# Attention and a gated MLP on one core: the attention weights are transposed under a second name typed fp32r

## The chip, the core and the metric

The program runs on one core of a Trainium2 chip. The metric is device time in microseconds (us) of one execution; lower is better. Engines are named as in the profile: PE is the matrix engine (TensorE), PEld its weight loads, DVE the vector engine, ACT the scalar engine, POOL is GpSimd, SP is the queue that issues DMAs.

## The reference

For 8 batches of 8 heads, with 576 positions and 64 dimensions a head, causal attention with a decay bias is computed, and the heads of a batch then go through a gated MLP:

```
scores = q @ k.T / sqrt(D)
cum    = cumsum(maximum(s, 0))
scores = where(causal, -1e9, scores + minimum(-(cum[i] - cum[j]), 0))
attn   = exp(scores - max(scores)); attn /= attn.sum() + 1e-9
x      = attn @ v                          # [8, 576, 512], heads side by side
h      = gelu(x @ w_in)                    # 512 -> 1024
u, v   = h[..., :512], h[..., 512:]
v_n    = layer_norm(v) * g_ln
out    = x + (u * (w_sg @ v_n + b_sg)) @ w_out
```

## The kernel before, in words

One head after the other goes through four steps, and the MLP of batch b is spread over the steps of the heads of batch b+1, so that PE has work of two kinds at any time.

1. *Scores* (L297 and L298 for heads 8 to 63, L295 for the first eight): five strips of query rows, `it` = 0 to 4, of 64, 192, 320, 448 and 576 columns, land in PSUM (`sc`). DVE adds the mask, scales, finds the row minimum and writes the strip to the SBUF tile `p_it` (L305). ACT takes the exponential in place and sums the row (L315).
2. *Normalization* (L338): POOL multiplies each strip by the reciprocal of its row sum, in place. Two small pieces go elsewhere: strip 0 (64x64) is written into columns 384 to 448 of `p_3`, and a 64x64 piece of strip 1 into columns 256 to 320 of `p_2`. For heads 0 to 11 ACT does strip 3 (L336).
3. *Transposes* (L377): PE transposes the strips in 13 pieces of 128x128 (one of them 128x64) into PSUM tiles `pt`, as four groups of 4, 4, 2 and 3. The data is the stationary operand and the identity moves: the profile writes `pt<-ident,p`. ACT (L88) and DVE (L93) take each group out of PSUM, as an fp32r high part and an fp32r rest (`pah`, `pal`, `pbh`, `pbl`, `pdh`, `pdl`). There are two sets of `p` tiles, for even and odd heads.
4. *Weights times values* (L450, L472; `xx`), added up by ACT and DVE into `xr`.

The MLP consists of units: `v` (L518, and L532 to L535 for the last 64 positions, which need the tile `xq` that a DMA copies from `xs`), `u` (L582), `s` (L597 to L601) and `o` (L616). All products are made of three fp32r products (high times high, high times rest, rest times high), except in the first 8 and 12 heads, where scores and values are plain fp32.

The order in which the steps are written is set by a table of times (`place`, `spread`). The order in which instructions then stand on each engine is set by the scheduler of the tile framework, which goes by its own estimates of durations; every engine runs its instructions in that order. The scheduler also places the waits: an instruction that reads a tile waits for the writers of what it reads.

Of the kernel before, what the change touches and what calls it, by code (L numbers as in the profile page):

```python
# [8 lines left out]
F32 = mybir.dt.float32  # L9
F32R = mybir.dt.float32r  # L10
# [10 lines left out]
P = 128  # L21
# [15 lines left out]
ITW = [64, 192, 320, 448, 576]  # L37
PW = [64, 192, 384, 512, 576]
# [21 lines left out]
def tile_attn_gmlp(  # L60
# [10 lines left out]
    out: bass.AP,  # L71
):
    nc = tc.nc

    const = ctx.enter_context(tc.tile_pool(name="const", bufs=1))
    att = ctx.enter_context(tc.tile_pool(name="att", bufs=2))
# [9 lines left out]
    def split(hi, lo, src, eng_hi, eng_lo):  # L86
        if eng_hi is nc.scalar:
            nc.scalar.copy(out=hi, in_=src)  # L88
        elif eng_hi is nc.gpsimd:
            nc.gpsimd.tensor_scalar(out=hi, in0=src, scalar1=1.0, scalar2=1.0, op0=ALU.mult, op1=ALU.mult)  # L90
        else:
            nc.vector.tensor_copy(out=hi, in_=src)
        eng_lo.tensor_tensor(out=lo, in0=src, in1=hi.bitcast(F32), op=ALU.subtract)  # L93
# [43 lines left out]
    for c0, n in ((0, 512), (512, REM)):  # L137
        ps = ps_sc.tile([P, 512], F32, name="cps", tag="sc")
# [10 lines left out]
    for i in range(WARM):  # L149
# [4 lines left out]
    nc.sync.dma_start(out=cum.rearrange("a h s -> h a s"), in_=cc[0:BH].bitcast(F32))  # L154


    ident = const.tile([P, P], F32, name="ident")
    nc.vector.memset(ident, 0.0)
    nc.gpsimd.affine_select(out=ident, in_=ident, pattern=[[1, P]], base=0, channel_multiplier=-1,
                            compare_op=ALU.not_equal, fill=1.0)  # L160
    mask = const.tile([P, 448], BF16, name="mask")
    nc.vector.memset(mask, 0.0)
# [4 lines left out]
    for r0, c in ((0, 512), (64, 448)):  # L167
        nc.gpsimd.affine_select(out=mask2[r0:r0 + 64, :], in_=mask2[r0:r0 + 64, :], pattern=[[-1, S]], base=c,
                                channel_multiplier=1, compare_op=ALU.is_ge, fill=NEG)
# [3 lines left out]


    q2 = []
    pbuf = []
    sums = []
    for i in range(2):
        t = const.tile([66, S], F32R, name=f"q2_{i}")
        nc.vector.memset(t[64:66, :].bitcast(F32), 1.0)  # L180
        q2.append(t)
        ts_ = []
        for it in range(5):
            t = const.tile([P, PW[it]], F32, name=f"p_{i}_{it}")
            if PW[it] > ITW[it]:
                nc.gpsimd.memset(t[:, ITW[it]:PW[it]], 0.0)
            ts_.append(t)
        pbuf.append(ts_)
        t = const.tile([P, 5], F32, name=f"sum_{i}")
        nc.vector.memset(t, 1.0)  # L190
        sums.append(t)
# [178 lines left out]

    def transposes(h):
        d = heads[h]
        pb = pbuf[h % 2]
        pt = {}

        def tr(ps, c, it, jb, n=P):
            nc.tensor.transpose(out=ps[0:n, c:c + P], in_=pb[it][:, jb:jb + n], identity=ident)  # L377

        def new(name, w):
            if h < NP:  # L380
                x = "hl"[h % 2]
                pt[name] = (att.tile([P, w], F32, name=name + x, tag=name + x, bufs=1),)
            else:
                pt[name] = tuple(att.tile([P, w], F32R, name=name + x, tag=name + x, bufs=1) for x in "hl")

        def evac(name, c0, ps, w, e=nc.scalar):
            if h < NP:
                o = pt[name][0][:, c0:c0 + w]
                (e.copy if e is nc.scalar else e.tensor_copy)(out=o, in_=ps[:, 0:w])  # L389
            else:  # L390
                hi, lo = (t[:, c0:c0 + w] for t in pt[name])
                split(hi, lo, ps[:, 0:w], nc.scalar, nc.vector)

        d["pt"] = pt
        t = ps_pt.tile([P, 512], F32, name="pt", tag="pt")
        for c, it in ((128, 3), (384, 2), (0, 1), (256, 4)):
            tr(t, c, it, 0)
        new("pa", 512)
        evac("pa", 0, t, 512)
        yield 0.43  # L400
        t = ps_pt.tile([P, 512], F32, name="pt", tag="pt")
        tr(t, 384, 3, 128)
        tr(t, 0, 3, 256)
        tr(t, 256, 2, 256)
        tr(t, 128, 4, 256)
        new("pb", 768)
        evac("pb", 0, t, 512, nc.vector)
        yield 0.43
        t = ps_pt.tile([P, 512], F32, name="pt", tag="pt")
        tr(t, 128, 2, 128)  # L410
        tr(t, 0, 4, 128)
        evac("pb", 512, t, 256)
        yield 0.43
        t = ps_pt.tile([P, 512], F32, name="pt", tag="pt")
        tr(t, 0, 4, 512, 64)
        tr(t, 64, 3, 384)
        tr(t, 192, 4, 384)
        if h < NP:
            pt["pd"] = (att.tile([P, 320], F32, name="pdh", tag="pdh", bufs=1),)
            nc.vector.tensor_copy(out=pt["pd"][0][0:64, 0:64], in_=t[0:64, 0:64])  # L420
            nc.vector.tensor_copy(out=pt["pd"][0][:, 64:320], in_=t[:, 64:320])
        else:
            hi, lo = pt["pd"] = tuple(att.tile([P, w], F32R, name="pd" + x, tag="pd" + x, bufs=1)
                                      for x, w in (("h", 320), ("l", 192)))
            nc.scalar.copy(out=hi[0:64, 0:128], in_=t[0:64, 0:128])
            nc.scalar.copy(out=hi[:, 128:320], in_=t[:, 128:320])
            nc.vector.tensor_tensor(out=hi[64:128, 0:128], in0=t[0:64, 0:128], in1=hi[0:64, 0:128].bitcast(F32),
                                    op=ALU.subtract)
            nc.vector.tensor_tensor(out=lo, in0=t[:, 128:320], in1=hi[:, 128:320].bitcast(F32), op=ALU.subtract)
        yield 0.35  # L430
# [205 lines left out]
    def advance(g, h):  # L636
        if h not in g[1]:
            g[1][h] = g[0](h)
        next(g[1][h], None)

    sc, tr, pp = (scores, {}), (transposes, {}), (pv, {})
    for h in range(BH):
        if h > 0:
# [25 lines left out]
    while steps:  # L669
        steps.sort()  # L670
        _, _, f, args = steps.pop(0)
# [53 lines left out]
```

## Time and profile before

| | |
|---|---|
| three timed runs | 827.47, 827.79, 828.27 us; median 827.79 |
| span of the profiled execution | 828.8 us, 1.0 us above that median |
| mean granted TensorE clock | 0.991 |
| PE busy | 792.6 us (96%) |
| DVE, ACT, POOL busy | 597.9 (72%), 576.5 (70%), 595.1 (72%) |
| L377, the transposes, on PE | 137.2 us in 832 instructions |

A PE record of a matmul is longer than the time that the matmul holds PE, since matmuls are pipelined; so the records overlap, and what a matmul costs a busy PE is read from the distance of the starts, or from the chain of waits, which gives each piece its share of the elapsed time. The chain follows back from the last instruction, at each step to whatever ended last.

### The profile page before, as it was taken

The numbers are of one execution on the slowest core, as the hardware profiler recorded it, in microseconds if no ns is written. First come the engines' busy times: TensorE is split into PE (matmuls) and PEld (weight loads), VectorE is DVE, ScalarE is ACT, GpSimd is POOL, SyncE is SP. The second block draws the span as 40 slices with busy tenths as digits, with TensorE's granted clock in tenths as the row PEclk, the third lists the DMA queues.
The fourth block names the chain that finished last, engine by engine and source line by source line (L and its number), as shares of the span: only waits on it lengthen the run. The fifth ranks groups of instructions, "written<-read, shape, count | busy, mean of one in ns | idle before, by whom it ended". The sixth has DMA issues, their size and how long they took to land.

```text
span 828.8 us, 16733 instructions
## 1 busy us (share of the span) xinstructions
PE 792.6 (96%) x5161; PEld 696.1 (84%) x5161; DVE 597.9 (72%) x1806; ACT 576.5 (70%) x1620; POOL 595.1 (72%) x979
## 2 busy tenths in 40 slices
PE   6899999899999999999989999999999999999878
PEld 3355666889989998999979998899989998899778
DVE  5995468975787578966888577965888678963652
ACT  4787778775686678866878577866787677862430
POOL 4987668878677768796768778785778778872451
PEclk9999999999999999999999999999999999999989
DMA  7656553343442543444434453443444353400101
GB/s 210 215 158 181 148 139 84 86 105 100 116 106 74 128 125 86 108 121 126 112 82 104 115 139 90 113 109 96 119 119 103 100 152 93 98 26 23 35 8 57
DMA packets 69804, 89.29 MB, mean 108 GB/s; under 512 B 25954, under 2 KB 42212, under 8 KB 69716
## 3 DMA queue, kind: packets, MB, share of 16 engines
q1 hardware_dynamic: 69716, 88.23, 40.8%
q8 instruction: 41, 0.67, 0.4%
q14 instruction: 47, 0.39, 0.2%
HBM read 42.27 MB, written 9.73 MB: 63 GB/s over the span
## 4 chain that ended last, share of the span: by engine, by line
PE 73%; DVE 12%; DMA 5%; ACT 3%; issue 3%; POOL 2%; SPq 1%; DVEq 0%; POOLq 0%; ACTq 0%
PE om L616 12%; PE sm L597 11%; PE um L582 10%; PE xx L450 10%; PE vm L518 9%; PE pt L377 8%; PE sc L297 4%; PE sc L298 4%; DVE p L305 2%; DMA xq<-xs 2%; DMA q<-k 2%; PE sm L601 1%; PE sm L600 1%; DVE wbits L220 1%; DVE vm L504 1%
## 5 line engine op out<-in xcount | busy, mean ns | idle before, releaser
L338 POOL TENSOR_SCALAR p<-p,rs 128x448 f32<-128x448 f32 (+4 forms) x372 | 180.5, 499 | 29.1 <-DVE rs L321 9.6
L315 ACT ACTIVATE p<-p,mn 128x448 f32<-128x448 f32 (+4 forms) x320 | 177.9, 557 | 24.5 <-DVE mn L305 22.4
L305 DVE CUSTOM_DVE_ANT_0 p<-sc,mask 64x64 f32<-64x64 f32 (+4 forms) x320 | 126.2, 422 | 56.4 <-PE pt L377 31.0
L377 PE MATMUL pt<-ident,p 128*128 128x128 f32 (+1 forms) x832 | 137.2, 278 | 5.3 <-DVE pbl L389 2.6
L597 PE MATMUL sm<-ws,vn 128*128 128x288 f32 x768 | 130.3, 304 | 0.7 <-POOL vn L567 0.6
L93 POOL TENSOR_TENSOR k<-raw,k 128x576 fp32r<-128x576 f32 x56 | 80.3, 1433 | 66.7 <-ACT k L88 33.3
L582 PE MATMUL um<-xs,wi 128*128 128x288 f32 x768 | 123.4, 300 | 2.5 <-DVE u L504 2.4
L616 PE MATMUL om<-gt,wo 128*128 128x288 f32 x768 | 125.7, 298 | 0.0
L582 PEld LDWEIGHTS um<-xs,wi 128*128 128x128 f32 x768 | 108.9, 188 | 8.9 <-DVE u L504 4.0
L597 PEld LDWEIGHTS sm<-ws,vn 128*128 128x128 f32 x768 | 112.4, 192 | 3.3 <-DVE u L504 1.0
L377 PEld LDWEIGHTS pt<-ident,p 128*128 128x128 f32 (+1 forms) x832 | 96.8, 138 | 21.8 <-DVE pbl L389 5.4
L616 PEld LDWEIGHTS om<-gt,wo 128*128 128x128 f32 x768 | 110.6, 188 | 2.3
L518 PE MATMUL vm<-wi,xs 128*128 128x512 f32 x384 | 103.4, 399 | 0.0
L297 PE MATMUL sc<-k,q 128*128 128x448 f32 x336 | 100.8, 308 | 1.5 <-DVE mn L305 0.8
L298 PE MATMUL sc<-k,q 66*128 66x448 f32 x336 | 89.3, 298 | 0.6 <-DMA k<-cum 0.6
L88 ACT CAST pbh<-pt 128x512 fp32r<-128x512 f32 x104 | 48.9, 479 | 58.8 <-PE pt L377 58.8
L518 PEld LDWEIGHTS vm<-wi,xs 128*128 128x128 f32 x384 | 69.7, 189 | 14.9 <-POOL xs L93 1.6
L93 POOL TENSOR_TENSOR gt<-u,gt 128x288 fp32r<-128x288 f32 x64 | 50.7, 806 | 41.6 <-ACT gt L88 41.1
L297 PEld LDWEIGHTS sc<-k,q 128*128 128x128 f32 x336 | 60.8, 181 | 9.1 <-DVE mn L305 3.9
L93 DVE TENSOR_TENSOR pbl<-pt,pbh 128x512 fp32r<-128x512 f32 x104 | 56.5, 549 | 15.9 <-ACT pbh L88 15.9
L298 PEld LDWEIGHTS sc<-k,q 66*128 66x128 f32 x336 | 60.9, 181 | 5.9 <-issue 0.9
L88 ACT CAST k<-raw 128x576 fp32r<-128x576 f32 x56 | 37.6, 671 | 39.5 <-PE sc L297 33.8
(142 smaller groups left out, 1704.8 us busy)
## 6 DMA issues: line engine op xcount, KB each, us to landing
q<-k SPq DMA_DIRECT2D x168, 144.0 KB
raw<-in_kq SPq DMA_DIRECT2D x56, 288.0 KB
vr<-in_vp SPq DMA_DIRECT2D x52, 192.0 KB
out_t<-ot SPq DMA_DIRECT2D x64, 144.0 KB
k<-k SPq DMA_DIRECT2D x56, 144.0 KB
wraw<-in_w_in SPq DMA_DIRECT2D x16, 256.0 KB
kf<-in_kq SPq DMA_DIRECT2D x8, 288.0 KB
qf<-in_kq SPq DMA_DIRECT2D x8, 288.0 KB
```

Of the source, the lines that this page charges most:

```text
L88: nc.scalar.copy(out=hi, in_=src)
L93: eng_lo.tensor_tensor(out=lo, in0=src, in1=hi.bitcast(F32), op=ALU.subtract)
L297: nc.tensor.matmul(o, d["q1"][:, i0:i0 + r], d["k1"][:, j0:j1], start=True, stop=False)
L298: nc.tensor.matmul(o, q2[h % 2][:, i0:i0 + r], d["k2"][0:66, j0:j1], start=False, stop=True)
L305: nc.vector.tensor_tensor_reduce(out=pbuf[h % 2][it][0:r, j0:j1], in0=pst[0:r, c0:c0 + j1 - j0], in1=(mask2 if it in (2, 4) else mask)[0:r ...
L315: nc.scalar.activation(out=p, in_=p, func=AF.Exp, bias=d["mn"][0:r, it:it + 1], scale=-1.0, accum_out=sums[h % 2][0:r, it:it + 1])
L338: e.tensor_scalar(out=po, in0=pi, scalar1=f, scalar2=1.0, op0=ALU.mult, op1=ALU.mult)
L377: nc.tensor.transpose(out=ps[0:n, c:c + P], in_=pb[it][:, jb:jb + n], identity=ident)
L518: nc.tensor.matmul(ps[0:r], xs[c][:, xi, ts_], wi[:, c, wj, fs], start=(n == 0), stop=(n == 11))
L582: nc.tensor.matmul(ps[:, 0:CH], wi[:, c, wj, dt * P:(dt + 1) * P], xs[c][:, xi, cs], start=(n == 0), stop=(n == 11))
L597: nc.tensor.matmul(ps[:, 0:CH], vn[j][:, vi, ds_], ws[:, j, wj, cs], start=(n == 0), stop=False)
L616: nc.tensor.matmul(ps[:, 0:CH], wo[:, c, wj, ms], gt[ch, c][:, gi, :], start=(n == 0), stop=(n == 11))
```

## The change

The `p` tiles leave the pool. They get fixed addresses in SBUF, in one reserved block, and each address range is declared twice: as `p_i_it` of type fp32, which DVE, ACT and POOL write and read as before, and as `r_i_it` of type fp32r, which the transposes read. The identity is declared fp32r and the transposes write their PSUM tile through an fp32r view, so that all three operands have one type. The PSUM tile itself keeps its fp32 type for those who read it.

```
+    pbuf, rbuf = [], []
+    at = (nc.sbuf_base + 31) // 32 * 32
+    nc.alloc_sbuf_tensor("p_all", [P, 2 * sum(PW)], F32)
+    for i in range(2):
+        ts_, rs_ = [], []
+        for it in range(5):
+            ts_.append(nc.alloc_sbuf_tensor_at(f"p_{i}_{it}", [P, PW[it]], F32, offset=at).ap())
+            rs_.append(nc.alloc_sbuf_tensor_at(f"r_{i}_{it}", [P, PW[it]], F32R, offset=at).ap())
+            at += 4 * PW[it]
+        pbuf.append(ts_)
+        rbuf.append(rs_)
...
-    ident = const.tile([P, P], F32, name="ident")
+    ident = const.tile([P, P], F32R, name="ident")
...
     def transposes(h):
         d = heads[h]
-        pb = pbuf[h % 2]
+        pb = rbuf[h % 2]
...
         def tr(ps, c, it, jb, n=P):
-            nc.tensor.transpose(out=ps[0:n, c:c + P], in_=pb[it][:, jb:jb + n], identity=ident)
+            nc.tensor.transpose(out=ps[0:n, c:c + P].bitcast(F32R), in_=pb[it][:, jb:jb + n], identity=ident)
```

Seven lines are added to the file, so L338 is L345 in the changed kernel, L377 is L384 and so on. No instruction is added or taken away on any engine; the scheduler, however, puts them in another order from the second head on, on all engines. Two places follow.

On PE, in the batch whose MLP runs beside heads 34 and 35, around the last 64 positions of the `v` unit; `xq` is the tile that the DMA brings, `um` is a `u` unit, `pal`, `pbh` are the transposed weights of head 34. Before:

```order
L450 MATMUL xx<-pal,vs 128x512
L532 MATMUL vm<-wi,xq 128x512
L533 MATMUL vm<-wi,xs 64x512
L582 MATMUL um<-xs,wi 128x288 x7
L532 MATMUL vm<-wi,xq 128x512
L533 MATMUL vm<-wi,xs 64x512
L582 MATMUL um<-xs,wi 128x288 x5
L450 MATMUL xx<-pbh,vs 128x448
L377 MATMUL pt<-ident,p_4_153 64x128
L377 MATMUL pt<-ident,p_3_151 128x128
L377 MATMUL pt<-ident,p_4_153 128x128
L532 MATMUL vm<-wi,xq 128x512
```

And in the changed kernel at the same place:

```order
L457 MATMUL xx<-pal,vs 128x512
L539 MATMUL vm<-wi,xq 128x512
L540 MATMUL vm<-wi,xs 64x512
L539 MATMUL vm<-wi,xq 128x512
L540 MATMUL vm<-wi,xs 64x512
L304 MATMUL sc<-k_5856,q_5858 128x288
L305 MATMUL sc<-k_5857,q_0_165 128x288
L457 MATMUL xx<-pbh,vs 128x448
L539 MATMUL vm<-wi,xq 128x512
L540 MATMUL vm<-wi,xs 64x512 x2
L589 MATMUL um<-xs,wi 128x288 x12
```

The seven products of the `u` unit that stood between the first two products with `xq` now stand behind the third one, with their five fellows. The same move is found once more, in batch 6.

On POOL, the normalization of head 30 (L338; even head, tiles of set 0). Before:

```order
L338 TENSOR_SCALAR p_3_151<-p_3_151,rs 128x448
L338 TENSOR_SCALAR p_2_149<-p_2_149,rs 128x320
L338 TENSOR_SCALAR p_1_148<-p_1_148,rs 128x128
L338 TENSOR_SCALAR p_4_153<-p_4_153,rs 128x576
L93 TENSOR_TENSOR xs<-xr,xs 128x576
L93 TENSOR_TENSOR gt<-u_4547,gt 128x288
L338 TENSOR_SCALAR p_3_151<-p_0_147,rs 64x64
L338 TENSOR_SCALAR p_2_149<-p_1_148,rs 64x64
```

And in the changed kernel:

```order
L345 TENSOR_SCALAR p_3_61<-p_3_61,rs 128x448
L345 TENSOR_SCALAR p_2_59<-p_2_59,rs 128x320
L345 TENSOR_SCALAR p_1_57<-p_1_57,rs 128x128
L345 TENSOR_SCALAR p_4_63<-p_4_63,rs 128x576
L105 TENSOR_TENSOR gt<-u_4405,gt 128x288
L105 TENSOR_TENSOR gt<-u_4932,gt 128x288
L105 TENSOR_TENSOR xs<-xr,xs 128x576 x2
L345 TENSOR_SCALAR p_3_61<-p_0_55,rs 64x64
L345 TENSOR_SCALAR p_2_59<-p_1_57,rs 64x64
```

Four pieces of MLP work instead of two stand between the last large strip and the two small writes. The waits differ as well. Before, a transpose waits for the writers of the columns that it reads: the first group of a head (columns 0 to 128 of each strip) waits for the four large writes alone, the second group for the small ones. In the changed kernel the second name is tracked as a whole tile: the first transpose of `r_3` waits for the small write into `p_3`, that of `r_2` for the small write into `p_2`.

More of the change, by code (lines that the diff above doesn't have):

```diff
@@ L154, in tile_attn_gmlp @@
     nc.sync.dma_start(out=cum.rearrange("a h s -> h a s"), in_=cc[0:BH].bitcast(F32))
-    ident = const.tile([P, P], F32, name="ident")
-    nc.vector.memset(ident, 0.0)
-    nc.gpsimd.affine_select(out=ident, in_=ident, pattern=[[1, P]], base=0, channel_multiplier=-1,
+    ident = const.tile([P, P], F32R, name="ident")
+    nc.vector.memset(ident.bitcast(F32), 0.0)
+    nc.gpsimd.affine_select(out=ident, in_=ident.bitcast(F32), pattern=[[1, P]], base=0, channel_multiplier=-1,
                             compare_op=ALU.not_equal, fill=1.0)
@@ L175, in tile_attn_gmlp @@
     q2 = []
-    pbuf = []
     sums = []
@@ L181, in tile_attn_gmlp @@
         q2.append(t)
-        ts_ = []
         for it in range(5):
-            t = const.tile([P, PW[it]], F32, name=f"p_{i}_{it}")
             if PW[it] > ITW[it]:
-                nc.gpsimd.memset(t[:, ITW[it]:PW[it]], 0.0)
-            ts_.append(t)
-        pbuf.append(ts_)
+                nc.gpsimd.memset(pbuf[i][it][:, ITW[it]:PW[it]], 0.0)
         t = const.tile([P, 5], F32, name=f"sum_{i}")
```

## The prediction

> **What bounds the kernel.** I read the head of the page and the chain of waits first, then the chain and the busy times by stage, then the chain at one place piece by piece.
>
> ```profile
> span 828.8 us, 16733 instructions
> PE 73%; DVE 12%; DMA 5%; ACT 3%; issue 3%; POOL 2%; SPq 1%; DVEq 0%; POOLq 0%; ACTq 0%
> ...
> by line: PE om L616 14.8%; PE sm L597 12.6%; PE um L582 11.7%; PE vm L518 10.5%; PE xx L450 10.3%; PE pt L377 10.0%; PE sc L297 5.1%; PE sc L298 5.1%; DMA xq<-xs 1.8%; DMA q<-k 1.7%; DVE p L305 1.5%; PE sm L601 1.4%; PE sm L600 1.2%; issue
> by line: PE xx L450 10.3%; issue 7.2%; PE pt L377 5.4%; DVE wbits L220 5.1%; DVE p L305 4.3%; PE vm L518 4.1%; PE sm L597 3.9%; PE um L582 3.8%; DVE wbits L222 3.4%; PE sc L297 3.1%; DMA wraw<-in_w_in 2.8%; PE sc L298 2.8%; POOL p L338 2.5%
> ...
> 180.00:760.00 580.00, 572.16 (x3975) 534.10 (x3974) 433.65 (x1320) 424.51 (x1194) 436.54 (x715) 1.00 0.40 103
> ```
>
> The first line of shares is the chain of the whole run. The two that follow are its shares by line between 180 and 760 us, and between 0 and 180 us. The last row is the busy time by engine from 180 to 760 us (PE, PEld, DVE, ACT, POOL, then clock, DMA share, GB/s). From 180 to 760 us PE's lines fill 82.7% of the chain (the ten PE entries added), while DVE, ACT and POOL are busy 75%, 73% and 75%: the stage is bound by PE. Before 180 us it is not: the seven PE entries there make 33.4%, and DVE, DMAs and issue time hold much of the rest. After 760 us no transposes are left. The transposes hold 10.0% of 580 us, 58.0 us, in the middle stage and 5.4% of 180 us, 9.7 us, in the early one: 67.7 us in all.
>
> **What a transpose costs now, and what it could cost.**
>
> ```profile
> 400.74 0.44 PE pt L377 x4
> 401.17 0.23 PE xx L450
> ...
> 402.99 0.22 PE pt L377 x2
> 403.21 0.23 PE xx L450
> 403.44 1.60 PE um L582 x12
> 405.05 0.33 PE pt L377 x3
> 405.37 0.21 PE xx L450
> 405.58 2.79 PE vm L518 x12
> ...
> 410.60 0.03 PE x L472
> 410.63 0.24 PE xx L450 x2
> ...
> 86.71 1.00 PE xx L450 x2
> ```
>
> These are pieces of the chain (start, length, what), with nothing waited for between them. A transpose takes 0.11 us in each group (0.44/4, 0.22/2, 0.33/3). The fp32r products beside it give the price of a column: 288 columns take 1.60/12 = 0.133 us, 512 take 2.79/12 = 0.2325 us, so 224 columns more cost 0.099 us, 0.44 ns each. The identity has 128 columns: one pass at the pace of fp32r is 0.133 - 160 x 0.00044 = 0.062 us. The row of 0.03 us, for 64 columns, lies on the same line (0.034). So a transpose typed fp32 holds PE for nearly twice one fp32r pass. The last row is a product typed fp32 with 512 columns in one of the first heads: 1.00 us, against 0.23 us for the 512 columns typed fp32r at 401.17. What is typed fp32 is thus dearer on PE in every row, and what is typed fp32r runs one pass even at 64 columns.
>
> The other side of a transpose is its weight load:
>
> ```profile
> L582 PEld LDWEIGHTS um<-xs,wi 128*128 128x128 f32 x768 | 108.9, 188 | 8.9 <-DVE u L504 4.0 <-DVE mn L305 0.8 <-issue 0.5
> L377 PEld LDWEIGHTS pt<-ident,p 128*128 128x128 f32 x768 | 90.7, 140 | 13.1 <-ACT p L336 1.1 <-DVE xr L479 1.1 <-DVE pbl L389 1.0
> ```
>
> A transpose's load is recorded with 140 ns, 48 ns less than that of an ordinary 128-column load. If the fp32r form keeps the short load, it stays below the 0.062 us of the pass. If it has the ordinary load, the three products at 410.60 set the pace: 64, 192 and 64 columns, each with an ordinary load, in 0.27 us, 0.09 us each, where the columns alone would take 0.158 us.
>
> **The change, part by part.**
>
> *The type of the transposes.* Bounds: 0.034 us (the 64-column row; nothing with 128 columns can be expected below it) to 0.11 us (no change). I take 0.062 us, because every fp32r row lies on that line and none shows a second pass. Each transpose on the chain then gives back 0.048 of 0.110 us, 44%: 25.3 us of the 58.0 in the middle stage and 4.2 us of the 9.7 in the early one, 29.5 us together. If instead all 832 gained, as with a chain that took in those now off it, it would be 39.9 us.
>
> The Trainium skill ("TensorE: Matmul & The Clock Gate", Terms) says that the transpose mode makes fp32 four times faster. Scaled to 128 columns the fp32 row above makes 0.25 us, so this trace shows 2.3 times; four times would be 0.062 us and would leave the new type nothing to gain, but no row here has a transpose that short.
>
> *Order on PE at the products with `xq`.*
>
> ```profile
> PE vm L532 <- DMA xq<-xs: 4.6, 4, 1.8
> ...
> 417.17 1.08 PE L582 MATMUL um<-xs,wi 128*128 128x288 f32 x7
> 420.07 0.50 PE L532 MATMUL vm<-wi,xq 128*128 128x512 f32 x1 [1.82 <-DMA xq<-xs]
> ```
>
> PE already waited here, 1.8 us at the longest, although seven `um` products (7 x 0.133 = 0.93 us) stood ahead. Where the change puts them behind, in batches 3 and 6, the wait grows by up to 0.93 us each: between 0 and 1.9 us, taken at 1.9 since the DMA is late now and a faster PE arrives sooner. Behind this wait stand the scores of the next head, so DVE and ACT are held as well.
>
> *The wait for the small writes.*
>
> ```profile
> 360.59 1.43 POOL L93 TENSOR_TENSOR xs<-xr,xs 128x576 fp32r<-128x576 f32 x1
> 361.98 0.80 POOL L93 TENSOR_TENSOR gt<-u,gt 128x288 fp32r<-128x288 f32 x1
> 362.76 0.71 POOL L338 TENSOR_SCALAR p<-p,rs 64x64 f32<-64x64 f32 x2
> 362.95 0.55 PE L377 MATMUL pt<-ident,p 128*128 128x128 f32 x3
> ...
> 393.45 1.45 POOL L338 TENSOR_SCALAR p<-p,rs 128x576 f32<-128x576 f32 x3
> 398.49 0.66 PE L377 MATMUL pt<-ident,p 128*128 128x128 f32 x4
> ```
>
> These are rows of the timeline for heads 30 and 33 (start, length). In head 33 the small writes end at 394.90, 3.6 us before the first transpose: the wider wait is free there, and so it is in most heads; what covers it is the lead of POOL over PE. In head 30 they end at 363.47, 0.5 us after the first transpose began, and in the changed order two more pieces, 0.80 and 1.43 us, stand ahead of them: up to 2.7 us late. Such a head comes once in eight (30, 38, 46, 54, 62). What is queued behind a waiting transpose on PE is the next scores and MLP products, so the wait is PE's whole. Bounds: 0 (the scheduler knows the wait and puts other products ahead) to 5 x 2.7 = 13.5 us. I take 0.5 us for each of the five, 2.5 us: nearer the lower end, as the order was made with this wait in it.
>
> *The rest.* In the early stage the transposes share the chain with DVE, DMAs and issue time; a third of the 4.2 us, 1.5 us, I count as lost to them. DVE, ACT and POOL get a middle stage that is some 4% shorter and rise from 75% to 78%: none becomes the bound; next late are the DMAs `xq<-xs` and `q<-k` (1.8% and 1.7% of the chain). Who takes the transposes out of PSUM reads the same fp32 tile with the same instructions: nothing. The second names, the fixed addresses and the retyped identity add no instruction: nothing, with no cover needed.
>
> *Sum.* 828.8 - 29.5 + 1.9 + 2.5 + 1.5 = 805.2 us of the profiled execution; the runs' median, 827.8, is 1.0 us below its span, so 804 us.
>
> **The rivals.**
>
> *Paced by the load.* If the fp32r transpose has the ordinary 188 ns load, it costs 0.09 us and not 0.062: 18% of 67.7 us, 12.3 us, less 1.9, 2.5 and 0.6: 828.8 - 7.3 - 1.0 = 820 us. For it: ordinary loads of fp32 and fp32r alike are long. Against it: the short load belongs to the transposes, not to a type.
>
> *The type does nothing.* The transposes keep their 0.11 us and the wider wait is covered: 828 us, give or take the new order.
>
> ```profile
> L377 PE MATMUL pt<-ident,p 128*128 128x128 f32 (+1 forms) x832 | 137.2, 278 | 5.3 <-DVE pbl L389 2.6
> ```
>
> For it: 278 ns is recorded for each, which could be mostly latency, and both types are four bytes wide. Against it: the starts are 0.11 us apart, so latency is not what they cost. The same page of the Trainium skill (Part 4) takes the side of this rival: some 275 ns for a transpose, most of it access latency, and a clock gate that a transpose does not engage. The record agrees with its 275 ns, the starts and the granted clock of 1.00 in the middle stage do not.
>
> *Slower: the wait for the small writes.* If the transposes keep their pace, nothing pays for the wait on POOL. With 2.5 us, and 1.9 us at `xq`, it is 832 us, with 13.5 us it is 843. It decides from the point where a transpose gains less than 4.4 us in 67.7, that is, costs above 0.103 us. With transposes at 0.062 us it would have to exceed 26 us, twice its bound.
>
> **How the numbers follow.** Forecast 0.62, load-paced 0.12, no effect 0.12, slower 0.14. The forecast's own range is 793 us (the chain's 29.5 us and half of the 10.4 us that lie off it, nothing given back) to 815 us (the wait at 13.5 us, `xq` and the early loss as taken). To hold 8 in 10, the range must take in the load-paced case and that without effect, and the lower part of the slower one: 793 to 830 us. It leaves out a twelfth of the forecast and more than half of the slower case, under 2 in 10. A change of 0.2%, 1.7 us, is about what can be told from no change here. Faster: the forecast, the load-paced case and a fifth of that without effect, where the order may help: 0.77. Slower: the slower case and a fifth of that without effect: 0.16. The same: 0.07.
>
> **What would show it.** If right, four transposes take about 0.25 us in the chain instead of 0.44, the share of L384 in the chain of the middle stage falls from 10.0% to about 6%, the records of transposes shorten from 278 ns by about the 0.05 us that the pass loses, and PE's waits for `xq` and for POOL's small writes grow by a few us together. Load-paced: four in 0.36 us, with loads recorded at 188 ns. No effect: four in 0.44 us. The forecast is wrong too if the transposes do shorten and the span does not follow; then PE's idle time will have risen by as much, and the waits name for what.

## The result, and the profile after

The changed kernel takes 851.59 us (median of four runs, 850.64 to 854.89), the kernel before 828.03 us beside it (827.47 to 829.14): ratio 1.0298, 95% interval 1.026 to 1.0336. It is 3% slower; 804 us were predicted.

The page of the changed kernel: span, clock in 40 slices, shares of the chain of waits by engine and by line, and the two groups of the transposes (busy time, mean ns of one, idle time before them and what ended it).

```profile
span 850.2 us, 16757 instructions
...
PEclk9899989789999999999999999999999999999989
...
PE 66%; DVE 10%; DMA 8%; ACT 8%; POOL 4%; issue 3%; SPq 1%; POOLq 0%; DVEq 0%; ACTq 0%
...
L384 PE MATMUL pt<-ident,r 128*128 128x128 f32 (+1 forms) x832 | 109.4, 248 | 9.1 <-ACT pah L396 3.6
...
L384 PEld LDWEIGHTS pt<-ident,r 128*128 128x128 f32 (+1 forms) x832 | 91.9, 140 | 29.5 <-DVE mn L312 5.9
```

The busy times by stage (PE, PEld, DVE, ACT, POOL, then clock, DMA share, GB/s), and the beginning of the chain's shares by line from 180 to 780 us:

```profile
0.00:140.00 140.00, 120.40 (x530) 71.39 (x531) 89.44 (x300) 94.99 (x275) 96.16 (x151) 0.95 0.57 158
140.00:180.00 40.00, 32.07 (x183) 28.21 (x181) 31.73 (x86) 28.86 (x82) 29.24 (x48) 0.79 0.38 94
180.00:780.00 600.00, 582.70 (x4057) 538.85 (x4057) 447.74 (x1352) 434.04 (x1219) 445.44 (x733) 0.99 0.40 102
...
by line: PE om L623 13.7%; PE sm L604 11.9%; PE um L589 10.6%; PE vm L525 9.5%; PE xx L457 9.1%; PE pt L384 5.9%; PE sc L304 4.7%; PE sc L305 4.3%; issue 2.5%; ACT p L322 1.9%; DMA vnr<-vnr 1.8%; DVE p L312 1.8%; PE sm L608 1.4%; DMA q<-k 1
```

The type took effect: the records of the transposes fall from 278 to 248 ns, and their share of the middle stage's chain falls from 10.0% to 5.9%, as forecast. The time did not follow. PE's share of the chain drops from 73% to 66%, and the clock between 140 and 180 us is 0.79.

Three of PE's longest waits in the changed kernel (us in total, times, longest); the longest of all, 5.9 us for `sp` at the start, is the same in both kernels:

```profile
PE sc L304 <- DMA k<-k: 5.6, 4, 2.1
PE vm L539 <- DMA xq<-xs: 4.5, 5, 1.7
...
PE pt L384 <- ACT pah L396: 3.6, 3, 2.0
```

The first and the last of these are not among the kernel before's waits. The waits for `xq` did not grow (4.6 us before), and no transpose waits for POOL's small writes anywhere. The head of the page counts 24 instructions more than before (16757 and 16733): they only wait for semaphores, and the matmuls and the work of the other engines are the same in number.

By the trace's starts, the first transpose of head 16 comes 15.4 us later than before, the stretch from there to the first transpose of head 63 takes 572.4 us instead of 564.2, and the remainder is 2.1 us shorter: 21.4 us of span. The experiments ask where each part comes from; most keep the order of instructions and change one thing.

### The profile page after: what moved, and what is told of

The parts are those of the page before. It is cut to its first block, busy times and chain, and to the rows that moved or that the text cites. A ratio compares the mean times of both kernels' runs of the same rounds, so it can differ in the third digit from the quotient of the medians.

```text
span 850.2 us, 16757 instructions
## 1 busy us (share of the span) xinstructions
PE 795.5 (94%) x5161; PEld 695.1 (82%) x5161; DVE 601.8 (71%) x1806; ACT 578.2 (68%) x1620; POOL 594.6 (70%) x979
## 4 chain that ended last, share of the span: by engine, by line
PE 66%; DVE 10%; DMA 8%; ACT 8%; POOL 4%; issue 3%; SPq 1%; POOLq 0%; DVEq 0%; ACTq 0%
PE om L623 11%; PE sm L604 9%; PE um L589 9%; PE vm L525 9%; PE xx L457 9%; PE pt L384 5%; PE sc L304 4%; PE sc L305 4%; DMA q<-k 2%; ACT p L322 2%; DVE p L312 2%; DMA wraw<-in_w_in 2%; DMA vnr<-vnr 1%; PE sm L608 1%; POOL p L345 1%
## 5 line engine op out<-in xcount | busy, mean ns | idle before, releaser
L345 POOL TENSOR_SCALAR p<-p,rs 128x448 f32<-128x448 f32 (+4 forms) x372 | 178.8, 494 | 31.3 <-DVE rs L328 18.7
L312 DVE CUSTOM_DVE_ANT_0 p<-sc,mask 128x448 f32<-128x448 f32 (+4 forms) x320 | 125.2, 422 | 54.6 <-PE pt L384 33.1
L589 PE MATMUL um<-xs,wi 128*128 128x288 f32 x768 | 127.6, 308 | 3.6 <-DVE u L511 3.1
L604 PE MATMUL sm<-ws,vn 128*128 128x288 f32 x768 | 125.2, 302 | 1.2 <-POOL vn L574 1.1
L589 PEld LDWEIGHTS um<-xs,wi 128*128 128x128 f32 x768 | 113.7, 197 | 8.4 <-DVE u L511 4.7
L384 PE MATMUL pt<-ident,r 128*128 128x128 f32 (+1 forms) x832 | 109.4, 248 | 9.1 <-ACT pah L396 3.6
L384 PEld LDWEIGHTS pt<-ident,r 128*128 128x128 f32 (+1 forms) x832 | 91.9, 140 | 29.5 <-DVE mn L312 5.9
L604 PEld LDWEIGHTS sm<-ws,vn 128*128 128x128 f32 x768 | 110.2, 191 | 3.1 <-POOL vn L574 1.5
L525 PE MATMUL vm<-wi,xs 128*128 128x512 f32 x384 | 105.3, 404 | 0.0
L105 POOL TENSOR_TENSOR vs<-vr,vs 128x384 fp32r<-128x384 f32 x52 | 53.5, 1029 | 20.4 <-ACT vs L100 17.1
```

Source lines behind the costliest of these rows:

```text
L312: nc.vector.tensor_tensor_reduce(out=pbuf[h % 2][it][0:r, j0:j1], in0=pst[0:r, c0:c0 + j1 - j0], in1=(mask2 if it in (2, 4) else mask)[0:r ...
L345: e.tensor_scalar(out=po, in0=pi, scalar1=f, scalar2=1.0, op0=ALU.mult, op1=ALU.mult)
L384: nc.tensor.transpose(out=ps[0:n, c:c + P].bitcast(F32R), in_=pb[it][:, jb:jb + n], identity=ident)
L525: nc.tensor.matmul(ps[0:r], xs[c][:, xi, ts_], wi[:, c, wj, fs], start=(n == 0), stop=(n == 11))
L589: nc.tensor.matmul(ps[:, 0:CH], wi[:, c, wj, dt * P:(dt + 1) * P], xs[c][:, xi, cs], start=(n == 0), stop=(n == 11))
L604: nc.tensor.matmul(ps[:, 0:CH], vn[j][:, vi, ds_], ws[:, j, wj, cs], start=(n == 0), stop=False)
```

## Experiments

### The order of one kernel with the type of the other

After the scheduler has set order and waits, the 832 transposes are replaced by the same instruction with other types (code shortened). In the first run the order and the waits are those of the kernel before and the type is fp32r; in the second they are those of the changed kernel and the type is fp32.

```
+def retyped(nc, names, dtype):
...
+    if type(i).__name__ == "InstMatmult" and i.is_transpose:
+        mov, x = i.ins
+        name = names.get(x.memref, x.memref)      # a second name at the same address
+        ins = [copy.replace(mov, dtype=dtype, ...), copy.replace(x, dtype=dtype, memref=name, ...)]
+        i = copy.replace(i, ins=ins, outs=[copy.replace(i.outs[0], dtype=dtype, ...)])
```

> The order and the waits of the kernel before on every engine, and only the 832 transposes typed fp32r (through a second name that is put in after scheduling). Theory O (the new order and waits cost the time, the type gains what was forecast): 795 to 812 us, faster than before by 2 to 4%. Theory T (the fp32r transposes themselves cost, for instance because PE's clock is granted less): 840 us or more, with a mean clock near the 0.974 of the changed kernel. If the type did nothing at all: 828 us.

> The order and the waits of the changed kernel on every engine, and the 832 transposes typed fp32 again. Theory O: slower still than the changed kernel, 860 to 880 us, since the order stays and PE has 832 x 0.03 to 0.048 us more to do. Theory T: back near 828 us.

Old order, new type: 820.55 us (seven runs, 818.62 to 822.46), ratio 0.9902 [0.9871, 0.9933]. New order, old type: 850.70 us, ratio 1.0281 [1.0232, 1.033], no different from the changed kernel. Theory T is out, but neither time is the one that theory O gave (795 to 812 and 860 to 880 us): the type is a gain of 1.0% in the old order and of nothing in the new one. The loss comes wholly with the order and the waits. The first of the two is the fastest version of this study, faster than both kernels.

The type gains 8 us where 29.5 were forecast. The chain of that first run, in a place with the same groups of transposes as those quoted from before (start, length, what):

```profile
398.10 0.30 PE pt L377 x4
398.39 0.30 PE xx L450
...
400.28 0.12 PE pt L377 x2
400.40 0.30 PE xx L450
...
402.30 0.21 PE pt L377 x3
402.51 0.27 PE xx L450
```

The groups shrink from 0.44, 0.22 and 0.33 us to 0.30, 0.12 and 0.21, but the product behind each of them grows from 0.23, 0.23 and 0.21 us to 0.30, 0.30 and 0.27. Group and follower together: 0.67 to 0.60, 0.45 to 0.42, 0.54 to 0.48, that is 0.16 us for nine transposes, 0.018 each, so 0.092 us in place of 0.11. The share of a line in the chain fell as forecast, and more than half of what it lost moved to the line behind. With 0.018 us of 0.11, the 67.7 us of transposes on the chain would give back 11 us (an estimate), near the 8 us measured.

### The pace of a transpose by itself

Six bursts of 48 instructions on PE at the start of the kernel before; their results are not read, the rest is unchanged (code shortened).

```
+    for i in range(48): nc.tensor.transpose(out=b1[:, 0:128].bitcast(F32R), in_=xr_, identity=idr)            # L166
+    for i in range(48): nc.tensor.transpose(out=b2[0:64, 0:128].bitcast(F32R), in_=xr_[:, 0:64], identity=idr) # L169
+    # L172, L175: the same two in fp32;  L178, L181: ordinary fp32r products with these operands
```

> The kernel before with six bursts of 48 independent PE instructions put in ahead of the first scores, all with 128 columns moving: transposes typed fp32r with 128 columns of weights (L166) and with 64 (L169), transposes typed fp32 with 128 (L172) and 64 (L175), ordinary fp32r products with 128 (L178) and 64 (L181). Theory L (an fp32r transpose is paced by its weight load): L166 0.085 to 0.09 us each, L169 0.055 to 0.065; L172 and L175 both 0.107, paced by the two passes of the moving operand. Theory M (paced by the moving operand and slowed by something else in the kernel): L166 and L169 both about 0.06. L178 0.107 or so, if an ordinary load takes longer than a transposing one.

The timeline of PE (start, us, what; `128*64` is a load of 64 columns), then the loads' groups (busy, mean ns of one):

```profile
11.63 4.19 PE L166 MATMUL b<-ident,sp 128*128 128x128 f32 x48
15.66 3.08 PE L169 MATMUL b<-ident,sp 128*64 128x128 f32 x48
18.58 5.41 PE L172 MATMUL b<-ident,st 128*128 128x128 f32 x48
23.82 5.40 PE L175 MATMUL b<-ident,st 128*64 128x128 f32 x48
28.98 5.55 PE L178 MATMUL b<-ident,sp 128*128 128x128 f32 x48
34.38 3.08 PE L181 MATMUL b<-ident,sp 128*64 128x128 f32 x48
...
L178 PEld LDWEIGHTS b<-ident,sp 128*128 128x128 f32 x48 | 5.4, 192 | 0.0
L172 PEld LDWEIGHTS b<-ident,st 128*128 128x128 f32 x48 | 5.2, 141 | 0.0
L166 PEld LDWEIGHTS b<-ident,sp 128*128 128x128 f32 x48 | 4.2, 140 | 0.1
```

From burst to burst, 48 fp32 transposes take 5.24 us (18.58 to 23.82), 0.109 each, and with half the load columns 5.16 us, 0.108: the size of the load does not set their pace. 48 fp32r transposes take 4.03 us, 0.084 each, and with half the load columns 2.92 us, 0.061. So the fp32r transpose keeps the short load, as the prediction argued, and is paced by it all the same: 0.061, very nearly the 0.062 us of the forecast, is reached only when the load has 64 columns. An ordinary fp32r product with 128 load columns takes 5.40 us, 0.112 each: it moves as many columns and writes as many rows as the transpose of L166, and its load is recorded with 192 ns instead of 140. With 64 load columns product and transpose both take 0.061 us (L181 runs from 34.38 us to the start of the next instruction at 37.29). So what goes with the pace at 128 columns is the load.

The Trainium skill ("TensorE: Matmul & The Clock Gate", Back-to-back issue gap) says that in a stream of load and matmul pairs both set the spacing, about 81 ns for 128 columns. The fp32r transposes agree (84 ns), the ordinary fp32r products do not (112 ns).

### The wait alone

The order and the type of the kernel before, but the first group of transposes of each head also waits for POOL's small writes; beside it the same with fp32r.

```
+def wide(nc):                      # after scheduling
...
+    v = max(small[k][2 * j:2 * j + 2])        # POOL's count when both small writes of head are done
+    w[w.index(q[0])] = copy.replace(q[0], wait_value=max(v, q[0].wait_value))
```

> Every engine's order and the fp32 type of the kernel before; only the first group of transposes of each head now waits, as in the changed kernel, until both small writes of POOL are done. In the profile of the kernel before, these writes end after the first transpose in heads 0, 1, 3, 10, 13 and 16 (by 2.17, 1.81, 0.97, 1.69, 0.17 and 3.00 us, 9.8 us together) and in heads 30, 38 and 46 (1.5 us together). Theory D (the wait itself costs what was lost before head 16): most of the 11.3 us shows, 836 to 840 us, and the first transpose of head 16 starts 8 to 10 us later than at 186.8 us. Theory O (the wait is cheap where the order is left alone; the loss comes from the order that the scheduler makes when it knows the wait): at most 3 us, 827 to 831 us, head 16 at 187 to 190 us.

> As the run beside it, with the transposes typed fp32r: the order of the kernel before with both things that the change brings, the type and the wait. Theory D: the type's gain of 8 us and the wait's loss of 8 to 11 us, 828 to 832 us. Theory O: 820 to 824 us, so that the change would have been a gain with the old order.

With the wait alone 839.26 us, ratio 1.0137 [1.012, 1.0154] to 827.99 us; with wait and type 835.82 us, 1.0096 [1.0069, 1.0124]. The first is what theory D gave; the second is 4 us above it, since the type gains 3.4 us here instead of 8. With the faster transposes PE waits for POOL for 13.0 us instead of 11.9, and the mean clock of the four runs is 0.978 to 0.985 instead of 0.986 to 0.994; no run separates the two. The wait itself is dear, though no engine's order has changed. PE's waits of the run with the wait alone:

```profile
PE pt L377 <- POOL p L338: 11.9, 10, 3.0
```

and of the kernel before:

```profile
PE pt L377 <- POOL p L338: 0.3, 2, 0.2
```

Six of the ten, with 9.5 us, stand before 200 us. Head 16 shows one. The timelines of POOL and PE in the kernel before:

```profile
182.63 1.50 POOL L338 TENSOR_SCALAR p<-p,rs 128x448 f32<-128x448 f32 x3
...
185.61 2.80 POOL L93 TENSOR_TENSOR xs<-xr,xs 128x576 fp32r<-128x576 f32 x2
188.36 0.82 POOL L93 TENSOR_TENSOR gt<-u,gt 128x288 fp32r<-128x288 f32 x1
189.15 0.71 POOL L338 TENSOR_SCALAR p<-p,rs 64x64 f32<-64x64 f32 x2
...
186.85 0.44 PE L377 MATMUL pt<-ident,p 128*128 128x128 f32 x2
```

and in the run with the wait:

```profile
193.96 0.72 POOL L338 TENSOR_SCALAR p<-p,rs 64x64 f32<-64x64 f32 x2
...
194.74 0.69 PE L377 MATMUL pt<-ident,p 128*128 128x128 f32 x2 [2.89 <-POOL p L338]
```

Before, the transposes of head 16 start at 186.85 us, while POOL is at MLP work until 189.15 us and at the small writes until 189.86, 3.0 us later. With the wait, PE stands still for 2.89 us until they end. By the start of head 16, 7.9 of the 11.0 us in span are lost, and 10.6 by head 20; after that the two kernels run in step (10.8 at head 63), though PE waits for POOL four more times, 2.3 us together. The 2.7 us between heads 16 and 20 are no wait for POOL: around the end of the wait of 2.89 us the granted clock falls, and it is 0.50 from 194 to 200 us, where the kernel before, at the same place (186 to 192 us), has 1.00. Half the clock over 6 us is worth up to 3 us (an estimate).

### The order that the scheduler makes

The transposes of the changed kernel never wait for POOL, and it is still 15.8 us slower than the old order with the same type and the same wait (851.59 and 835.82 us; 1.0298 and 1.0096, intervals apart). With fp32 in both it is 11.4 us (850.70 and 839.26). What is left to differ is the order, and the addresses of the `p` tiles. No run changed the addresses alone, but the instructions that use these tiles keep their mean durations: POOL's scaling 494 ns (499 before), ACT's exponential 558 (557), DVE's writing 422 (422), the transposes' loads 140 (138). So the rest lies in the order.

Two kernels with half of the change, each in the order that the scheduler gives it: the second name with type fp32 (wide waits, and the scheduler counts the old duration), and the `p` tiles in their pool, typed fp32r, with DVE, ACT and POOL writing through an fp32 view (narrow waits, new duration).

```
-            rs_.append(nc.alloc_sbuf_tensor_at(f"r_{i}_{it}", [P, PW[it]], F32R, offset=at).ap())
+            rs_.append(nc.alloc_sbuf_tensor_at(f"r_{i}_{it}", [P, PW[it]], F32, offset=at).ap())
```

```
-            t = const.tile([P, PW[it]], F32, name=f"p_{i}_{it}")
+            r = const.tile([P, PW[it]], F32R, name=f"p_{i}_{it}")
+            rs_.append(r)
+            t = r.bitcast(F32)
```

> The second name at fixed addresses, but typed fp32, with identity and PSUM view fp32 as before: the scheduler keeps the old prices and gets the new, whole-tile waits alone, and makes its own order. Theory W (the whole-tile waits of tensors outside the pools cost the time): 840 to 855 us. Theory S (it is the scheduler's price of the fp32r transposes that leads it to a worse order): 828 to 835 us.

> Pool tiles as before, so that a transpose waits only for the writers of its own columns, and transposes that the scheduler knows as fp32r: it makes its own order with the new prices and the old, narrow waits. Theory W: 795 to 812 us, the full gain of the type. Theory S: 835 to 855 us, as slow as the changed kernel, since the price misleads it in the same way.

846.93 us, 1.0237 [1.0195, 1.028], and 841.71 us, 1.0174 [1.0118, 1.023]: each time the slower of the two forecasts, theory W in the first and theory S in the second, so both halves cost. Either half makes a new order, and each of these is slower than the old order with the same waits and type: 846.93 against 839.26 us, and 841.71 against 820.55 us. The early stage divides by the wait: head 16 begins at 196.1 us in the first and at 186.4 in the second, close to where the old order with the same wait and type has it (194.7 and 186.3). The middle one does not: from the first transpose of head 16 to the last of head 63 it is 585.2 and 582.7 us, against 575.6 and 563.7 in the old order. So these two orders lose their time in the middle stage.

Was the old order a lucky one? `MT` is the number in the table of times that spreads an MLP's units over the heads (52.0). A shift by 0.5 changes neither the work nor its type nor the kind of the waits, only the order:

```
-MT = 52.0
+MT = 51.5
```

> The kernel before with one number of its table changed, MT from 52.0 to 51.5, which says how fast the MLP units are spread over the heads; no transposes, waits or types are touched, but the scheduler comes to another order on all engines (as many places differ as between the two kernels). Theory P (the order of before is a tuned point, and about any other order costs): 10 to 25 us slower than before, like the changed kernel. Theory C (the waits and the price that the change brings make its order a bad one): within 5 us of before.

> The changed kernel with MT at 51.5. Theory P: another draw from the same heap, 835 to 860 us. Theory C: stays at 845 to 860 us, since the waits and the price stay.

> The kernel before with MT at 52.5: a smaller change of the order (about a third as many places on PE). Theory P: 2 to 20 us slower than before. Theory C: within 5 us of before.

The kernel before with 51.5 takes 839.22 us, 1.015 [1.0119, 1.018], with 52.5 it takes 836.39 us, 1.0082 [1.0045, 1.012]. Both are what theory P gave. The changed kernel with 51.5 takes 852.01 us, 1.029 [1.0259, 1.0321], as with 52.0, which both theories allowed. So the order of the kernel before is better than its neighbours. Six other orders stand in these runs (the changed kernel's, the two halves', and three with a shifted `MT`); each is slower than the old order with the same waits and type, by 8 us (846.93 against 839.26) to 21 us (841.71 against 820.55), and a shift by 0.5 alone costs the kernel before 11.8 and 9.0 us against the 827.40 us beside it.

What in the new order costs the time is settled in part. Up to head 16 the changed kernel loses 7.6 us more than the old order with type and wait (202.2 and 194.6 us). Its busy row for 140 to 180 us stands above; this is that of the old order with type and wait:

```profile
140.00:180.00 40.00, 36.58 (x250) 31.62 (x248) 35.77 (x108) 33.75 (x98) 34.76 (x58) 1.00 0.41 101
```

In the same 40 us PE does 183 instructions instead of 250, at a mean clock of 0.79 instead of 1.00 (it is 0.50 throughout from 146 to 152 us and from 164 to 172). PE's gaps there are short, and each has another releaser (idle time before an instruction in brackets):

```profile
144.73 0.59 PE L304 MATMUL sc<-k,q 128*128 128x448 f32 x2 [2.13 <-DMA k<-k]
146.53 0.71 PE L305 MATMUL sc<-k,q 66*128 66x448 f32 x1 [1.22 <-POOL vs L105]
...
161.43 2.36 PE L589 MATMUL um<-xs,wi 128*128 128x288 f32 x12 [1.88 <-DVE u L511]
...
166.01 0.50 PE L384 MATMUL pt<-ident,r 128*128 128x128 f32 x2 [1.20 <-DVE pal L105]
```

From head 16 to head 63 the busy rows are, for the changed kernel:

```profile
202.20:774.60 572.40, 556.41 (x3880) 513.80 (x3878) 429.58 (x1295) 416.46 (x1172) 426.59 (x702) 1.00 0.41 104
```

and for the old order with type and wait:

```profile
194.60:755.90 561.30, 550.19 (x3861) 513.16 (x3861) 423.85 (x1291) 414.46 (x1164) 425.86 (x699) 0.99 0.41 105
```

That is 11.1 us more, at the full clock. PE is idle for 16.0 us (572.40 - 556.41) instead of 11.1. The other 6.2 us lie within PE's records. The changed order has 19 more instructions of PE in this stretch (3880 and 3861); at 561.30/3861 = 0.145 us each that is 2.8 us of them (an estimate), and behind head 63 the changed kernel is 1.7 us shorter. The remaining 3.4 us no run here took apart.

Nor was the clock varied by itself, so how much of the early 7.6 us is the clock and how much the gaps stays open. One pair bears on it: the kernel with the changed order and fp32 transposes runs the same instructions in the same order as the changed kernel. It reaches head 16 at 197.2 us, with a mean clock of 0.95 to that point; the changed kernel reaches it at 202.2 us, with 0.92. From there to head 63 it is the other way round, 577.6 against 572.4 us. So the type does gain 5.2 us in the middle stage, and 5.0 us are lost early, where the clock is lower. The mean clock of the runs goes the same way wherever the type gains less than its 8 us: 0.966 to 0.975 with fp32r and 0.984 to 0.988 with fp32 in the changed order, 0.978 to 0.985 and 0.986 to 0.994 in the old order with the wait.

## Why the prediction was wrong, step by step

Three steps failed: the size of the type's gain (21.5 us too large), the term of nothing for names, addresses and the new order (15.8 us), and the place and price of the wait (8.8 us). The type and the wait as measured already turn the gain into a loss of 8 us (835.82); the order adds the rest. Between the measured kernels the way goes +11.3 us (the wait), -3.4 (the type under that wait) and +15.8 (the order), a loss of 23.7 us where a gain of 24 was forecast; taken in another sequence the parts would have other sizes.

| step | predicted | measured |
|---|---|---|
| type of the transposes | -29.5 us | -8.0 us alone (820.55 against 828.51), -3.4 us with the wait, none in the changed order |
| order at `xq` | +1.9 us | 4.6 us of waits before, 4.5 after |
| wait for the small writes | +2.5 us, at most 13.5 | +11.3 us alone (839.26 against 827.99) |
| early loss of the type's gain | +1.5 of 4.2 us | 0.5 us gained by head 16, 3.7 lost |
| names, addresses, the new order | nothing | +15.8 us (851.59 against 835.82) |

*The type.* The step that failed is the choice of 0.062 us between the bounds 0.034 and 0.11. It read the cost off the moving columns alone, and that a short load "stays below the 0.062 us of the pass" rested on no row; the load sets the pace at 0.084 us in a burst, and in the kernel a transpose costs about 0.092. That four transposes would take 0.25 us in the chain did not come true either: they take 0.30. The rival "paced by the load" had 0.09 us. It tied that to a load of 188 ns and was set aside because the short load belongs to transposes: the record is indeed 140 ns, but a short load still paces a shorter pass. The rule of the Trainium skill that the prediction weighed ("TensorE: Matmul & The Clock Gate", Terms: the transpose mode makes fp32 four times faster) stays unsupported: the fp32 transpose takes 0.109 us, not 0.062. (The row of 1.00 us behind the 0.25 us reads x2: a plain fp32 product stands in the trace as two records, 120 for the 60 of the first twelve heads, and a transpose as one.) The rival "type does nothing" is wrong too: the interval of the type alone excludes no change.

*The wait.* Its place was misread. The step took heads 30, 38, 46, 54 and 62 as the only ones with late small writes, from rows of the middle stage. In the kernel before, the small writes ended after the first transpose in heads 0, 1, 3, 10, 13 and 16 as well, by 9.8 us together, where POOL has no lead over PE. With the 1.5 us of heads 30, 38 and 46 that is the measured 11.3 us, but the match is in part luck: 7.9 us are lost by head 16, 2.7 more between heads 16 and 20, where the clock is 0.50 for 6 us, and next to nothing at the later heads. The reason for the lower end, that the order was made with this wait in it, was right on the fact and wrong on the price: the scheduler did keep the transposes from waiting for POOL, and the order that it made with that wait and the new type was dearer than the wait (850.70 us against 839.26, both with fp32).

*The order.* That second names and a new type "add no instruction: nothing" left out 15.8 us. They add no instruction that works, but they change what the scheduler knows, the waits and a duration, and it set the order anew on every engine. The prediction priced two places that it could see in the order and gave the rest no term and no room in the range.

*The rival "slower"* had the sign and, with 832 to 843 us, the two causes that the old order shows (839.26 and 835.82 us lie in it). The changed kernel lies beyond it by the order. Its condition did not hold, though: it was to decide where a transpose costs above 0.103 us, and one costs 0.092. That its sign came true is in part luck. Among the signs named, the chain's share (5.9%) came true and the records shortened, by 0.03 us instead of 0.05; the last one, that the transposes shorten and the span does not follow, with PE's idle time risen, describes what happened: 36.2 us of the span before (828.8 - 792.6), 54.7 after (850.2 - 795.5).

## What to carry to other kernels

A change that adds no instruction can still cost by what it tells a scheduler: where the order was tuned, give the new order a term of its own, which in these runs was about 1 to 2.6%, and make the change after scheduling to see its bare worth. An instruction whose pass gets shorter can next be paced by its own load, as the transposes here were: take as its price the larger of the two, and add the follower's row when a share of the chain is read. To bound a wait that becomes wider, count the heads in which it would bite over the whole span, the ramp above all, rather than in a typical period.

## What the runs showed of the hardware

- In a burst, a transpose with 128 moving columns starts every 0.109 us in fp32 (0.108 with a 64-column load) and every 0.084 us in fp32r (0.061 with a 64-column load).
- Loads are quicker in a transpose than in an ordinary fp32r product with the same operands: 0.084 against 0.112 us from start to start, 140 against 192 ns in the records.
- The mean granted clock was 0.79 over 40 us in which PE's longest gap was 2.13 us and PE was busy for 32.07 us. In another run it was 0.50 for 6 us from the end of a single wait of 2.89 us on; the same stretch without the wait ran at 1.00.
